# Output projection in plain 4608-byte runs with its input re-placed by small copies, and V units evacuated in pairs, in a gated attention + MLP decode kernel

## The chip, the cores and the metric

The kernel runs on one core of a Trainium2 chip. The metric is the device time of one execution in microseconds, as a median of runs of the same kernel. The profile shown is of one execution on the same kind of core; its times are counted from the first instruction of the span.

## What is computed

For eight batch rows with one token each (D = 576), the reference mixes an attention branch and an MLP branch by a gate:

```python
g = _sigmoid((x * gate_w).sum(-1, keepdims=True))
# attention: 32 query heads, 16 K/V heads, last W = 2048 of 8192 positions, Dh = 128
q = (x @ wq).reshape(B, 1, 32, 128)
p = softmax(q . k[:, :, -W:, :] * Dh ** -0.5)
a = (p . v[:, :, -W:, :]).reshape(B, 1, 4096) @ wo
b = _gelu(layernorm(x) @ w1 + b1) @ w2 + b2      # F = 4608
return g * a + (1 - g) * b
```

All tensors are bf16. The K and V windows are 67 MB each, wq, wo, w1 and w2 some 20 MB together.

## The kernel before

All data lives in one SBUF arena, addressed by hand. Operations aren't emitted where they are written: `add` and `dma` only record them, with an engine, dependencies (`deps`: wait until done; `after`: not started earlier), a cost in us and a priority. `_Plan.schedule` (L62) is a list scheduler: among all operations whose predecessors are planned it takes the one with the smallest planned start minus 0.2 us per unit of priority, then the higher priority, then the earlier recorded. So each engine's instruction order is fixed before the run, from these costs, and at run time every engine works through its own list in order and waits on semaphores.

All large loads go through SP's queue in one fixed order, each behind the one before (`after=last_dma`). First wq and w1. Then the order string (L553) interleaves 16 K units (4 MB), 32 V units (2 MB) and the four chunks of wo; b2 and four chunks of w2 follow. A load waits for its buffer: K units alternate between slots 0-1 and 2-3, V units and w2 chunks go round slots 4 to 8, and wo's four chunks take slots 0 to 3 when K is through (L735).

A K unit (L629) holds 512 positions of 32 (batch, K/V head) rows: two batch rows with all 16 heads, which make a G. Its two halves are transposed by VectorE in 32x32 blocks (L652) into two KT buffers, and TensorE multiplies them by the queries (L664) into 32 rows of PSUM. After four K units (one G complete), two softmaxes (`softmax`, L582) run, g = 2G and 2G+1: a row maximum (L586), its merging over the four partition quadrants by tiny copies (L589 to L595), the exponential on ScalarE with row sums (L597), four masked copies (L604), four block transposes into PT (L612), and then the row sums: a diagonal (L615), a matmul that adds over partitions (L616), the reciprocal (L618) and the product with the gate, rg (L623).

A V unit (L680, `v_compute` L687) holds all 2048 positions of four (batch, K/V head) rows: heads n and n + 8 of two batch rows. `pv` (L695) makes 16 matmuls of 512 columns, cycling over four column tiles of 32, into one of two PSUM banks. ScalarE copies the bank to SBUF (`uev`, L704). A selection (`us`, L710), four fp32 matmuls against a piece of an identity matrix (each shows as two instructions), adds the tiles' diagonal blocks and leaves the output with the head dimension on partitions. Two units make an item: ScalarE copies its result (L720), and GpSimd (for the last item VectorE) multiplies by rg and writes oT (L731), laid out by K/V head.

The output is accumulated in one PSUM bank by groups (`AccGroup`, L535) of matmul pairs of 288 columns in two column tiles (L544): `project` (L744) takes oT against wo, `m2_chunk` (L758) the MLP's hidden values against w2. When all groups are done, VectorE and ScalarE each take half out of PSUM (L790, L791) and two small DMAs write it (L793).

The lines that the change and the prediction touch are `softmax`, `k_unit`'s end, `v_compute`, `wo_chunk`, `project`, `m2_chunk` and the loop over the stream.

Of the kernel before, what the change touches and what calls it, by code (L numbers as in the profile page):

```python
# [181 lines left out]
def build_kernel(nc, A_x, A_k_cache, A_v_cache, A_wq, A_wo, B_x, B_w1, B_b1, B_w2, B_b2, gate_w, out):  # L182
# [13 lines left out]
    FC, FJ = 4, 9  # L196
# [10 lines left out]
    with ExitStack() as es:  # L207
# [22 lines left out]
        req("sel", 4 * 128, BF)  # L230
# [3 lines left out]
        req("qT", 256, BF)  # L234
# [14 lines left out]
        req("EV", 2 * 512, F32)  # L249
        req("oT", Hkv * 16, BF)  # L250
# [12 lines left out]
        over("xg", "P", 0, D, F32)  # L263
        over("xc", "KT", 0, D, F32)
# [25 lines left out]
        i32 = view("i32")  # L290
        idf8 = view("idf8", 8)
# [20 lines left out]
        oT = view("oT").rearrange("p (u h b) -> p u h b", u=Hkv, h=2)  # L312
# [139 lines left out]
        o_i32 = []  # L452
        for q in range(4):
            o_i32.append(add("dve", (lambda q=q: lambda e: e.tensor_copy(i32[32 * q:32 * q + 32, :], ident[32 * q:32 * q + 32, 32 * q:32 * q + 32]))(),
                             deps=[o_ident, o_obl], name="i32_%d" % q, cost=0.15, prio=-1))
# [79 lines left out]
        class AccGroup:  # L535
            def __init__(self, name, mms, deps, cost, after=(), prio=0):
# [3 lines left out]
                def fn(e):  # L540
# [13 lines left out]
                 "w w v v w w v v v v v v")  # L554
        count = {"K": 0, "V": 0, "W": 0}
        stream = []
        for word in order.split():
            kind = "V" if word == "v" else "W" if word == "w" else "K"
            stream.append((kind, count[kind]))
            count[kind] += 1  # L560
        assert (count["K"], count["V"], count["W"]) == (NKU, NUQ, Hq // WO_CH)
        stream += [("B", 0)] + [("M", i) for i in range(FC)]
# [19 lines left out]
        def softmax(g):  # L582
# [16 lines left out]
            exp_done[g] = [ex]  # L599
            pms = []  # L600
# [14 lines left out]
            ds = add("dve", lambda e: e.tensor_scalar(out=dsum, in0=i32, scalar1=k(S), scalar2=None, op0=ALU.mult), deps=[ex] + o_i32 + ([rg_done[g - 1]] if g else []), name="ds_%d" % g, cost=0.16, prio=5)  # L615
            sp_ = add("pe", lambda e: e.matmul(ps[:, BK_S, 0:32], ones_f, dsum, start=True, stop=True), deps=[ds] + b6_r[-2:], after=b6_w[-1:], name="sum_pe%d" % g, cost=0.5, prio=5)  # L616
            b6_w.append(sp_)
            rc = add("dve", lambda e: e.reciprocal(out=rr, in_=ps[:, BK_S, 0:32]), deps=[sp_], name="rc_%d" % g, cost=0.16, prio=5)  # L618
            b6_r.append(rc)

            def rg_fn(e):
                in1 = bass.AP(arena_f, offset=foffs("gb") + 2 * (g // 2), ap=[[AST // 2, 128], [0, 4], [1, 2], [0, 4]])
                return e.tensor_tensor(out=rg[:, g % 2, :].rearrange("p (v b m) -> p v b m", v=4, b=2), in0=rr.rearrange("p (v b m) -> p v b m", v=4, b=2), in1=in1, op=ALU.mult)  # L623
            deps = [rc, o_gb]
            if g >= 2:
                deps.append(oT_done[4 * (g - 2) + 3])
            rg_done[g] = add("dve", rg_fn, deps=deps, name="rg_%d" % g, cost=0.16, prio=5)

        def k_unit(i):  # L629
# [18 lines left out]
            for h in range(2):  # L648
# [5 lines left out]
                         deps=deps, name="tr%d_%d" % (i, h), cost=5.0, after=tr_hist[-1:])  # L654
# [21 lines left out]
            if c == 3:  # L676
                softmax(2 * G)
                softmax(2 * G + 1)
# [8 lines left out]
        def v_compute(i, s, d):  # L687
            g, q = divmod(i, 4)
            item = 2 * g + q // 2

            def pv_fn(e):
                mm = None
                for t in range(16):
                    c = 32 * (t % 4)
                    mm = e.matmul(ps[c:c + 32, BK_OS[i % 2], :], PT[:, g % 2, 512 * q + 32 * t:512 * q + 32 * t + 32], slot(s)[:, 512 * t:512 * t + 512],  # L695
                                  start=(t < 4), stop=(t >= 12), skip_group_check=True, tile_position=(0, c))
                return mm
            deps = [d] + pt_done[g] + ([u_ev[i - 2]] if i >= 2 else o_qT + [o_u])
            prev = add("pe", pv_fn, deps=deps, name="pv%d" % i, cost=1.5, after=pv_hist[-1:])
            pv_hist.append(prev)  # L700
            slot_free[s] = [prev]
            if q == 3:
                pv_last[g] = prev
            u_ev[i] = add("act", lambda e: e.activation(out=EV[:, i % 2, :], in_=ps[:, BK_OS[i % 2], :], func=ACTF.Copy),  # L704
                          deps=[prev] + ([u_sum[i - 2]] if i >= 2 else [o_hT]), name="uev%d" % i, cost=0.8, prio=3)

            def us_fn(e):
                mm = None
                for r in range(4):
                    mm = e.matmul(ps[:, BK_S, OC + 16 * (item % 2) + 8 * (q % 2):OC + 16 * (item % 2) + 8 * (q % 2) + 8], EV[:, i % 2, 128 * r:128 * r + 128], i32[:, 8 * r:8 * r + 8],  # L710
                                  start=(r == 0), stop=(r == 3), skip_group_check=True)
                return mm
            u_sum[i] = add("pe", us_fn, deps=[u_ev[i]] + o_i32 + b6_r[-2:], after=b6_w[-1:], name="us%d" % i, cost=1.0, prio=3)
            b6_w.append(u_sum[i])
            if q % 2 == 1:
                hl = q // 2
                prev = u_sum[i]
# [8 lines left out]
                for t in (i - 1, i):  # L726
                    G, n = divmod(t, 8)

                    def om_fn(e, t=t, G=G, n=n):
                        dst = bass.AP(arena, offset=aoffs("oT") + 16 * n + 2 * G, ap=[[AST, 128], [1, 2], [128, 2], [8, 2]])  # L730
                        return e.tensor_tensor(out=dst, in0=src_[:, 8 * (t % 2):8 * (t % 2) + 8].rearrange("p (b l h) -> p b l h", b=2, l=2),  # L731
                                               in1=rg[:, g % 2, 8 * (t % 4):8 * (t % 4) + 8].rearrange("p (b l h) -> p b l h", b=2, l=2), op=ALU.mult)
                    oT_done[t] = add(eng, om_fn, deps=deps, name="oT%d" % t, cost=0.25, prio=9)

        def wo_chunk(i):  # L735
            s = i
            h0 = WO_CH * i
            dst = slot(s)[:, 0:WO_CH * WOP].rearrange("p (t c) -> p t c", t=WO_CH)
            d = dma("sp", lambda e: e.dma_start(dst[:, :, 0:D], A_wo[128 * h0:128 * (h0 + WO_CH), :].rearrange("(t p) c -> p t c", p=128)),
                    "s%d" % s, WO_CH * 128 * D * 2, deps=slot_free[s], name="d_wo%d" % i, after=last_dma[-1:])  # L740
            last_dma.append(d)
            wo_here.append((dst, d))

        def project():  # L744
            for n in range(8):
                for hkv in (n, n + 8):
                    dst, d = wo_here[2 * hkv // WO_CH]
                    mms = [(oT[:, hkv, h, :], dst[:, 2 * hkv % WO_CH + h, 0:D]) for h in range(2)]
                    AccGroup("proj%d" % hkv, mms, [oT_done[n + 8 * m] for m in range(4)] + [d], cost=0.5)
# [8 lines left out]
        def m2_chunk(ci):  # L758
# [5 lines left out]
            for n, (j0, j1) in enumerate(zip(cuts, cuts[1:])):  # L764
# [6 lines left out]
                ops.append(AccGroup("m2_%d_%d" % (ci, n), mms, [o_hT, d], cost=0.25 * (j1 - j0), after=o_m2[-1:]).op)  # L771
# [4 lines left out]
        v_here, wo_here = [], []  # L776
        for kind, i in stream:
# [3 lines left out]
            while v_here and v_here[0][0] // 4 in pt_done:  # L781
                v_compute(*v_here.pop(0))
# [74 lines left out]
```

## Time and profile before

| What | us |
|---|---|
| Median of 5 runs | 367.7 |
| Lowest and highest | 366.93, 370.26 |
| The profiled execution | 367.76 |
| Its span, first to last instruction | 366.5 |
| PE busy (matmul) | 259.9 |
| VectorE busy | 210.9 |
| ScalarE busy | 31.0 |
| GpSimd busy | 17.4 |

In the rows by slice, each figure stands for a fortieth of the span (9.2 us); a digit is a busy share in tenths. A group line gives a source line, an engine, an operation, its destination and source with their shapes, the count, then the busy time in us and the mean of one in ns, then how long the engine was idle just before and what ended that. PE is the matmul stream, PEld the loading of weights, SPq and ACTq the queues from which DMAs are issued, POOL is GpSimd. Clock 1.0 is the full TensorE clock and 0.5 half of it.

### The profile page before, as it was taken

The numbers are of one execution on the slowest core, as the hardware profiler recorded it, in microseconds if no ns is written. First come the engines' busy times: TensorE is split into PE (matmuls) and PEld (weight loads), VectorE is DVE, ScalarE is ACT, GpSimd is POOL, SyncE is SP. The second block draws the span as 40 slices with busy tenths as digits, with TensorE's granted clock in tenths as the row PEclk, the third lists the DMA queues.
The fourth block names the chain that finished last, engine by engine and source line by source line (L and its number), as shares of the span: only waits on it lengthen the run. The fifth ranks groups of instructions, "written<-read, shape, count | busy, mean of one in ns | idle before, by whom it ended". The sixth has DMA issues, their size and how long they took to land.

```text
span 366.5 us, 4165 instructions
## 1 busy us (share of the span) xinstructions
PE 259.9 (71%) x1805; PEld 133.9 (37%) x1805; DVE 210.9 (58%) x255; ACT 31.0 (8%) x69; POOL 17.4 (5%) x80
## 2 busy tenths in 40 slices
PE   0179684847589959466899293748999497368997
PEld 0169331312255424222544141213744233126555
DVE  0610986575997490869954442779854836960000
ACT  1010000000210000002100000002100100021110
POOL 4012000001000000010000000000000000000000
PEclk9999999669698967696969768586769788755579
DMA  9999999999999999999999999999999999999994
GB/s 403 429 425 410 426 431 449 415 446 415 445 424 434 426 431 440 424 445 413 451 420 436 426 433 424 443 418 442 420 452 422 442 379 436 401 432 433 426 427 181
DMA packets 12618, 154.58 MB, mean 422 GB/s; under 512 B 1036, under 2 KB 5300, under 8 KB 5816
## 3 DMA queue, kind: packets, MB, share of 16 engines
q1 hardware_dynamic: 12544, 154.29, 98.9%
q8 instruction: 14, 0.23, 0.2%
q10 hardware_dynamic: 56, 0.03, 0.0%
q14 instruction: 4, 0.03, 0.0%
HBM read 154.31 MB, written 0.01 MB: 421 GB/s over the span
## 4 chain that ended last, share of the span: by engine, by line
DMA 40%; PE 29%; DVE 28%; issue 1%; SPq 1%; ACT 1%; DVEq 0%
DMA arena<-in_A_k_cache_dram 35%; DVE arena L652 16%; PE ps L664 14%; PE ps L710 8%; DVE arena L612 6%; DMA arena<-in_A_v_cache_dram 4%; PE ps L695 4%; PE ps L544 2%; DVE arena L604 2%; DVE arena L586 1%; DVE arena L595 1%; DVE arena L589 1%; SPq L683 1%; ACT arena L704 1%; DVE arena L618 0%
## 5 line engine op out<-in xcount | busy, mean ns | idle before, releaser
L652 DVE STREAM_TRANSPOSE arena<-arena 128x4096 f32<-128x4096 f32 x32 | 141.1, 4431 | 84.7 <-DMA arena<-in_A_k_cache_dram 75.8
L664 PE MATMUL ps<-arena 128*32 128x512 bf16 x512 | 141.4, 441 | 37.0 <-DVE arena L652 36.9
L664 PEld LDWEIGHTS ps<-arena 128*32 128x32 bf16 x512 | 51.2, 105 | 118.8 <-DVE arena L652 43.0
L695 PE MATMUL ps<-arena 128*32 128x512 bf16 x512 | 57.0, 542 | 28.7 <-DMA arena<-in_A_v_cache_dram 15.7
L710 PE MATMUL ps<-arena 128*128 128x8 f32 x256 | 41.3, 293 | 6.8 <-ACT arena L704 3.3
L710 PEld LDWEIGHTS ps<-arena 128*128 128x128 f32 x256 | 39.1, 238 | 19.0 <-issue 6.8
L695 PEld LDWEIGHTS ps<-arena 128*32 128x32 bf16 x512 | 19.5, 123 | 50.5 <-issue 28.7
L612 DVE STREAM_TRANSPOSE arena<-arena 128x512 bf16<-128x512 bf16 x32 | 30.6, 1015 | 0.0
L704 ACT ACTIVATE arena<-ps 128x512 f32<-128x512 f32 x32 | 19.1, 596 | 124.8 <-PE ps L695 90.7
L731 DVE TENSOR_TENSOR arena<-ps,arena 128x8 bf16<-128x8 f32 x2 | 0.3, 188 | 30.4 <-PE ps L710 30.4
L731 POOL TENSOR_TENSOR arena<-arena 128x8 bf16<-128x8 f32 x30 | 5.8, 231 | 239.9 <-ACT arena L720 239.9
L597 ACT ACTIVATE arena<-ps,arena 128x512 bf16<-128x512 f32 x8 | 5.5, 688 | 115.2 <-DVE arena L595 115.2
L616 PE MATMUL ps<-arena 128*128 128x32 f32 x16 | 3.9, 334 | 12.8 <-DVE arena L615 12.8
L586 DVE TENSOR_REDUCE arena<-ps 128x1 f32<-128x512 f32 x8 | 5.5, 692 | 13.0 <-PE ps L664 12.9
L501 PE MATMUL ps<-arena 128*128 128x8 bf16 x144 | 10.9, 201 | 1.7 <-DMA arena<-in_B_w_dram 1.7
L544 PE MATMUL ps<-arena 128*8 128x288 bf16 (+1 forms) x140 | 12.0, 316 | 0.0
L501 PEld LDWEIGHTS ps<-arena 128*128 128x128 bf16 x144 | 10.8, 157 | 2.1 <-DMA arena<-in_B_w_dram 2.1
L645 POOL TENSOR_TENSOR arena<-arena 128x32 bf16<-128x32 bf16 x32 | 6.4, 239 | 81.0 <-PE ps L664 72.0
L604 DVE TENSOR_SCALAR arena<-arena 128x512 bf16<-128x512 bf16 x32 | 9.0, 345 | 1.0 <-ACT arena L597 0.8
L616 PEld LDWEIGHTS ps<-arena 128*128 128x128 f32 x16 | 3.0, 234 | 17.1 <-DVE arena L615 15.7
L419 PE MATMUL ps<-arena 8*128 8x8 bf16 x8 | 0.6, 171 | 11.9 <-DVE arena L392 7.9
L544 PEld LDWEIGHTS ps<-arena 128*8 128x8 bf16 (+1 forms) x140 | 6.1, 92 | 4.6 <-issue 2.2
(81 smaller groups left out, 78.0 us busy)
## 6 DMA issues: line engine op xcount, KB each, us to landing
arena<-in_A_k_cache_dram SPq DMA_DIRECT2D x16, 4096.0 KB, 23.9
arena<-in_A_v_cache_dram SPq DMA_DIRECT2D x32, 2048.0 KB, 23.8
arena<-in_B_w_dram SPq DMA_DIRECT2D x1, 4608.0 KB, 23.8
arena<-in_A_wo_dram SPq DMA_DIRECT2D x4, 1152.0 KB, 10.6
arena<-in_A_wq_dram SPq DMA_DIRECT2D x1, 4096.0 KB, 13.2
arena<-in_B_w_dram SPq DMA_DIRECT2D x3, 1296.0 KB, 14.5
arena<-in_B_w_dram SPq DMA_DIRECT2D x3, 576.0 KB, 9.3
arena<-in_A_wq_dram SPq DMA_DIRECT2D x1, 512.0 KB, 3.3
```

What stands on the lines that cost most here:

```text
L501: ins = e.matmul(out_, lhsT, yT[:, kt, :], start=(kt == 0), stop=False)
L544: ins = e.matmul(ps[32 * j:32 * j + 8, BK_ACC, 0:JN], lhsT, rhs[:, JN * j:JN * j + JN], start=False, stop=True, skip_group_check=True, til ...
L586: mx = add("dve", lambda e: e.tensor_reduce(out=k(MX), in_=ps[:, bank, :], axis=AXL.X, op=ALU.max), deps=[qk_done[g]], name="mx%d" % g, co ...
L604: return e.tensor_scalar(out=dst, in0=view("Pd").rearrange("p (s n) -> p s n", s=2), scalar1=amask[:, a:a + 1], scalar2=None, op0=ALU.mult)
L612: return e.transpose(dst, src)
L616: sp_ = add("pe", lambda e: e.matmul(ps[:, BK_S, 0:32], ones_f, dsum, start=True, stop=True), deps=[ds] + b6_r[-2:], after=b6_w[-1:], name ...
L645: return e.tensor_tensor(out=dst, in0=src, in1=own, op=ALU.mult)
L652: tr = add("dve", (lambda h=h, kb=kb: lambda e: e.transpose(bass.AP(arena_f, offset=foffs("KT") + kb * SE // 2, ap=[[AST // 2, 128], [4, 1 ...
L664: mm = e.matmul(ps[32 * c:32 * c + 32, 2 * (G % 2) + nb, :], qb[:, G % 2, n, 2 * h + ee, :], rhs, start=(h == 0 and t == 0), stop=(h == 1 ...
L695: mm = e.matmul(ps[c:c + 32, BK_OS[i % 2], :], PT[:, g % 2, 512 * q + 32 * t:512 * q + 32 * t + 32], slot(s)[:, 512 * t:512 * t + 512], st ...
L704: u_ev[i] = add("act", lambda e: e.activation(out=EV[:, i % 2, :], in_=ps[:, BK_OS[i % 2], :], func=ACTF.Copy), deps=[prev] + ([u_sum[i - ...
L710: mm = e.matmul(ps[:, BK_S, OC + 16 * (item % 2) + 8 * (q % 2):OC + 16 * (item % 2) + 8 * (q % 2) + 8], EV[:, i % 2, 128 * r:128 * r + 128 ...
```

## The change

Wo. A chunk's 1024 rows were read as 1152-byte rows, each partition taking one row from each of eight blocks of 128. Now partition p takes four consecutive rows (4608 bytes) from each of two blocks of 512, so that partition p's row j of block c is row 512 c + 4 p + j. The contraction over a head's 128 dimensions thus no longer lies with dimension on partitions, and the attention output has to be re-placed: the products are first written to oN, and 16 copies per step, one for each pair of partition quadrants, move pieces of 32 partitions into the new oT. One such step handles all that is there after unit 23, and one each follows units 25, 27, 29 and 31 (80 copies in all, on VectorE). The projection becomes 8 groups of four matmul pairs instead of 16 groups of two.

V. The two units of an item share a PSUM bank: the first takes column tiles 0 and 1, the second 2 and 3, so that each unit cycles over two tiles. One ScalarE copy, now reading PSUM with a stride, and one selection with 16 columns (against a new constant, i2) serve both.

Softmax. The row-sum operations are recorded ahead of the masked copies and transposes (now `spread`). Softmaxes go through a list, `waiting`. Some planned costs change, and qT and sel move into another buffer's space. The order of the stream stays the same.

```diff
-        req("sel", 4 * 128, BF)
+        req("i2", 64, F32)
...
+        req("oN", Hkv * 16, BF)
...
+        o_i20 = add("dve", lambda e: e.memset(view("i2"), 0.0), name="i2z", cost=0.1, prio=-1)
+        o_i2 = [add("dve", (lambda q=q: lambda e: e.tensor_copy(i2[32 * q:32 * q + 32, :, q // 2, :], ident[32 * q:32 * q + 32, 32 * q:32 * q + 32].rearrange("p (r m) -> p r m", r=4)))(),
+                    deps=[o_i20, o_ident], name="i2_%d" % q, cost=0.15, prio=-1) for q in range(4)]
...
             exp_done[g] = [ex]
+            ds = add("dve", lambda e: e.tensor_scalar(out=dsum, in0=i32, scalar1=k(S), scalar2=None, op0=ALU.mult), deps=[ex] + o_i32 + ([rg_done[g - 1]] if g else []), name="ds_%d" % g, cost=0.16, prio=5)
+            sp_ = add("pe", lambda e: e.matmul(ps[:, BK_S, 0:32], ones_f, dsum, start=True, stop=True), deps=[ds] + b6_r[-2:], after=b6_w[-1:], name="sum_pe%d" % g, cost=0.5, prio=5)
+            b6_w.append(sp_)
+            rc = add("dve", lambda e: e.reciprocal(out=rr, in_=ps[:, BK_S, 0:32]), deps=[sp_], name="rc_%d" % g, cost=0.16, prio=5)
+            b6_r.append(rc)
...
+        def spread(g):
+            ex = exp_done[g][0]
             pms = []
...
-                         deps=deps, name="tr%d_%d" % (i, h), cost=5.0, after=tr_hist[-1:])
+                         deps=deps, name="tr%d_%d" % (i, h), cost=4.5, after=tr_hist[-1:])
...
                 for t in range(16):
-                    c = 32 * (t % 4)
-                    mm = e.matmul(ps[c:c + 32, BK_OS[i % 2], :], PT[:, g % 2, 512 * q + 32 * t:512 * q + 32 * t + 32], slot(s)[:, 512 * t:512 * t + 512],
-                                  start=(t < 4), stop=(t >= 12), skip_group_check=True, tile_position=(0, c))
+                    c = 64 * (i % 2) + 32 * (t % 2)
+                    mm = e.matmul(ps[c:c + 32, bk, :], PT[:, g % 2, 512 * q + 32 * t:512 * q + 32 * t + 32], slot(s)[:, 512 * t:512 * t + 512],
+                                  start=(t < 2), stop=(t >= 14), skip_group_check=True, tile_position=(0, c))
                 return mm
-            deps = [d] + pt_done[g] + ([u_ev[i - 2]] if i >= 2 else o_qT + [o_u])
-            prev = add("pe", pv_fn, deps=deps, name="pv%d" % i, cost=1.5, after=pv_hist[-1:])
+            deps = [d] + pt_done[g] + ([u_ev[item - 2]] if item >= 2 else o_qT + [o_u])
+            prev = add("pe", pv_fn, deps=deps, name="pv%d" % i, cost=1.9, after=pv_hist[-1:])
...
+            if i % 2 == 0:
+                return
+            u_ev[item] = add("act", lambda e: e.activation(out=EV[:, item % 2, :], in_=ps[:, bk, :].rearrange("p (r d j) -> p r j d", r=4, j=4), func=ACTF.Copy),
+                             deps=pv_hist[-2:] + ([u_sum[item - 2]] if item >= 2 else [o_hT]), name="uev%d" % item, cost=1.2, prio=3)
...
-            u_sum[i] = add("pe", us_fn, deps=[u_ev[i]] + o_i32 + b6_r[-2:], after=b6_w[-1:], name="us%d" % i, cost=1.0, prio=3)
+            u_sum[item] = add("pe", us_fn, deps=[u_ev[item]] + o_i2 + b6_r[-2:], after=b6_w[-1:], name="us%d" % item, cost=1.9, prio=3)
...
+                if i == NUQ - 9:
+                    place(slice(0, 8), slice(0, 6), list(oT_done.values()))
+                elif i >= NUQ - 8:
+                    c = (i % 8) // 2
+                    place_done[c] = place(slice(c, 8, 4), slice(6, 8), [oT_done[i - 1], oT_done[i]])
+
+        place_done = {}
+
+        def place(ch, bs, deps):
+            return [add("dve", (lambda j=j, q=q: lambda e: e.tensor_copy(oT[32 * q:32 * q + 32, ch, j, bs], oN[32 * j:32 * j + 32, q, ch, bs]))(), deps=deps, name="pl%d%d" % (j, q), cost=0.1, prio=2)
+                    for j in range(4) for q in range(4)]
...
-            dst = slot(s)[:, 0:WO_CH * WOP].rearrange("p (t c) -> p t c", t=WO_CH)
-            d = dma("sp", lambda e: e.dma_start(dst[:, :, 0:D], A_wo[128 * h0:128 * (h0 + WO_CH), :].rearrange("(t p) c -> p t c", p=128)),
+            dst = slot(s)[:, 0:WO_CH * D].rearrange("p (c n) -> p c n", c=2)
+            src = A_wo[128 * WO_CH * i:128 * WO_CH * (i + 1), :].rearrange("(c p j) n -> p c (j n)", c=2, j=4)
+            d = dma("sp", lambda e: e.dma_start(dst, src),
...
-            for n in range(8):
-                for hkv in (n, n + 8):
-                    dst, d = wo_here[2 * hkv // WO_CH]
-                    mms = [(oT[:, hkv, h, :], dst[:, 2 * hkv % WO_CH + h, 0:D]) for h in range(2)]
-                    AccGroup("proj%d" % hkv, mms, [oT_done[n + 8 * m] for m in range(4)] + [d], cost=0.5)
+            for c in range(4):
+                for ch in (c, c + 4):
+                    dst, d = wo_here[ch // 2]
+                    mms = [(oT[:, ch, j, :], dst[:, ch % 2, D * j:D * j + D]) for j in range(4)]
+                    AccGroup("proj%d" % ch, mms, place_done[c] + [d], cost=1.0)
...
-                ops.append(AccGroup("m2_%d_%d" % (ci, n), mms, [o_hT, d], cost=0.25 * (j1 - j0), after=o_m2[-1:]).op)
+                ops.append(AccGroup("m2_%d_%d" % (ci, n), mms, [o_hT, d], cost=0.16 * (j1 - j0), after=o_m2[-1:]).op)
...
-            while v_here and v_here[0][0] // 4 in pt_done:
-                v_compute(*v_here.pop(0))
+            while True:
+                if waiting and (waiting[0] < 2 or waiting[0] - 2 in pv_last):
+                    softmax(waiting[0])
+                    spread(waiting.pop(0))
+                elif v_here and v_here[0][0] // 4 in pt_done:
+                    v_compute(*v_here.pop(0))
+                else:
+                    break
```

## The prediction

> **What bounds the kernel now.** I read the page first: span, the rows by slice, the queues.
>
> ```profile
> span 366.5 us, 4165 instructions
> ...
> DMA  9999999999999999999999999999999999999994
> GB/s 403 429 425 410 426 431 449 415 446 415 445 424 434 426 431 440 424 445 413 451 420 436 426 433 424 443 418 442 420 452 422 442 379 436 401 432 433 426 427 181
> ...
> q1 hardware_dynamic: 12544, 154.29, 98.9%
> ```
>
> The 16 DMA engines are busy 98.9% of the span with one queue, SP's, and the bytes (154 MB) don't change. Only three things can move the end: the rate at which bytes flow, a hole in the stream, and what follows the last byte. The GB/s row has two dips late, 379 and 401: there Wo is read. Busy time by stretch (columns: PE, PEld, DVE, ACT, POOL busy, PE clock, DMA share, GB/s) with Wo's second half in the first row and V loads in the second:
>
> ```profile
> 312.60:318.60 6.00, 1.31 (x5) 0.60 (x3) 5.65 (x20) 0.78 (x2) 0.00 (x0) 0.77 1.03 381
> 318.60:328.60 10.00, 6.07 (x50) 2.20 (x50) 8.21 (x22) 1.86 (x4) 0.00 (x0) 0.50 1.03 433
> ```
>
> The engines are equally busy and move 12% less. Then the end, in the chain of waits (start us, us, what):
>
> ```profile
> 353.11 0.61 ACT arena L704
> 353.71 0.04 issue
> 353.76 1.06 PE ps L710 x8
> ...
> 356.57 0.61 ACT arena L704
> 357.18 0.04 issue
> 357.22 1.06 PE ps L710 x8
> 358.28 6.29 PE ps L544 x96
> ...
> 364.59 0.45 DVE arena L790
> ```
>
> PE is the last link: 96 accumulation matmuls (L544) run without a gap from 358.28 to 364.57. The trace's landing times say that the last piece of w2 is there at 363.15. So PE ends 1.42 us behind the data, working off a backlog left by the last V units. Last, the prices:
>
> ```profile
> L664 PE MATMUL ps<-arena 128*32 128x512 bf16 x512 | 141.4, 441 | 37.0 <-DVE arena L652 36.9
> L695 PE MATMUL ps<-arena 128*32 128x512 bf16 x512 | 57.0, 542 | 28.7 <-DMA arena<-in_A_v_cache_dram 15.7
> L710 PE MATMUL ps<-arena 128*128 128x8 f32 x256 | 41.3, 293 | 6.8 <-ACT arena L704 3.3
> ```
> ```profile
> 312.23 0.49 DVE L589 COPY arena<-arena 32x1 f32<-32x1 f32 x3
> 320.27 3.60 PE L695 MATMUL ps<-arena 128*32 128x512 bf16 x32 [3.15 <-DVE arena L612]
> ```
>
> 57.0/32 = 1.8 us per V unit for L695, 41.3/32 = 1.3 us for L710. Three tiny DVE copies take 0.49, starts 0.175 apart.
>
> [...] a 1152-byte packet takes 51 ns, a 4608-byte one (in w2's last chunk) 178, not 204. [...] at full clock, sixteen 512-column matmuls over four column tiles (L695) take 1.04 us at 100.9, while eight in one tile (L664) take 1.98. [...] The clock records have just 0.5 and 1.0, in steps of 3.4 us; it rose at 309.0 in an unbroken run of L664, but stayed half from 315.8 to 353.4 although PE looked busy from 331 on, mixing L695 and L710. [...]
>
> **The change, part by part.** The sum is made against the profiled execution, 367.76 us (span 366.48 and 1.28 around it), 0.06 above the median of 367.7.
>
> *Wo in 4608-byte runs.* Packets 4096 -> 1024. By landing times, the four chunks add 12.1 us to the stream (K15 299.76, Wo 302.76 and 305.78; V25 315.47, Wo 318.48 and 321.55). A 589,824-byte piece of w2 in 4608-byte packets adds 1.38 us (360.03 to 361.41, again to 362.79); Wo holds eight such: 11.04. **Gain 1.04 us.** Packet durations give more, (4096 x 51 - 1024 x 178)/16 = 1.66 us, but packets overlap a little on an engine; landings decide, 1.66 stays as the other end. The stream is one fixed SP order, so all later landings move up by 1.04: V31 350.87 -> 349.8, last w2 piece 363.15 -> 362.1. Shorter descriptor lists also free SP's issue (V24's took 4.75 us, V26's 3.17, after Wo): worth nothing, 10.7 and 8.9 us were queued ahead.
>
> *PV in two column tiles per unit instead of four.* Eight rounds replace four: the eight-in-one-tile row L664 is the price, 1.98 us full clock, 3.62 half (1.04 and 1.90 before). 32 units: +30 us at full clock, +55 at half. *One evacuation and selection per pair*: 16 selections of 8 matmuls go, 16 x 1.06 = -17 us at full clock, -30 at half; 16 columns instead of 8 cost nothing, weights being loaded for 128 (PEld 238 ns of the 293). 16 evacuations of 0.60 us go. Net on PE +13 to +25 us in 366, where it is 71% busy; hidden in the body by DMA, and worth anything only where a slot is freed late. Smallest covers: K6 issued at 111.49 with 7.3 us still to land ahead, w2's last chunk at 353.10 with 6.9. Without cover each us late costs a us. The strided evacuation isn't in this trace: between 0.60 (same elements) and 1.20 (twice), below 0.60 excluded since as many elements are read; I take 0.60.
>
> *Row sums ahead of the masking.* The reciprocal now stands before the transposes on DVE and waits for a PE matmul that queues behind PV; behind it wait the mask products, transposes and K's next transpose, hence K's next load. Bound 0 to one or two PV units (3.6 us half clock each) per softmax, no gain on the path; covers above: zero. It also lets selection 12 go before the last transposes; in the profile it waited for the reciprocal at 327.66 and then behind V27's landing. New i2 operations run in DVE's empty first 30 us.
>
> *Placing.* 80 copies on DVE. The first 16, behind pair 11, fall near 299, where K15's transpose starts: 16 x 0.175 = 2.8 us late at most. That pushes Wo's third load (issued 308.58, 6.9 us of cover): zero. The last 16 stand in the tail: 2.8 us.
>
> *Tail.* V24 can start at about 321.0 (320.3, plus reciprocal and product ahead of the transposes). [...] PE then waits for V landings. After V31 (349.8): PV 2.8 (mean of both clocks), evacuation 0.7, selection 1.47 (mean of 1.06 and 1.88): 354.8. Then 0.14 to DVE, two products 0.27, copies 2.8, last projection 8 pairs x 0.12 = 1.0 and 0.1 of waits: 359.1. w2's third chunk lands at 359.0 and takes 1.1, the fourth's pieces land at 360.4, 361.75, 362.1: the second takes 0.5, the last pair 0.12 and 0.3 to end: **362.7**. Before 364.57: gain 1.87, of which 1.04 is DMA and 0.83 the backlog. What is late next is the data itself.
>
> 367.76 - 1.87 = **365.9 us**.
>
> **Rivals.** *Transfer only*: copies and PV keep PE as far behind as now; 367.76 - 1.04 = 366.7. For: 2.8 us of new copies in the tail. Against: 16 selection matmuls fewer there. *More*: packet times are right and the backlog goes with a full clock, 1.66 + 0.9: 365.2. *PE ends it* (slower): the clock stays half, as it did from 315.8 to 353.4. From 321.0, 8 PV x 3.62, 4 selections x 1.88, two evacuations x 0.7, and 22 accumulation pairs x 0.24 make 43.2 us; 32.4 are done by 353.4, the rest at full clock takes 5.4: selection 15 ends at 358.8. With 0.4 of products, 2.9 of copies and wait, 1.0 of projection and 2.5 for the two chunks: 365.6, +1.0, 368.8; the clock a window later adds 1.7: 370.5. Point 369.7. It decides from a selection that ends after 357.7. For: the clock row[...].
>
> **Numbers.** Forecast 0.48, its own range 365.2 to 366.6; transfer only 0.15; more 0.20; PE ends it 0.17. 0.5% of 367.7 is 1.84 us, about what a measurement of this kernel can tell from no change; the forecast lies on that line, so it splits: faster 0.25, same 0.23. With "more" faster, "transfer only" same, and "PE ends it" slower 0.15, same 0.02: 0.45, 0.40, 0.15. Range 364.8 (1.66, and the lag down from 1.42 to the 0.4 that the last two matmuls need, 365.1, less 0.3 for scatter between runs) to 368.9 (PE with the clock as before).
>
> **What would show it.** Four Wo loads of 4608-byte packets at about 427 GB/s; last landing about 362; PE's last run of L544 with gaps waiting for DMA; L695's busy time near 100 us, L710's near 21; sixteen DVE copies taking about 2.8 us before the last projection. Wrong if landings move by less than 0.7 or more than 1.7 us, if the DMA row shows a hole near Wo or w2, or if PE still runs its last matmuls without a gap.

## The result, and the profile after

| | before | changed |
|---|---|---|
| Median of runs | 367.8 (76 runs) | 366.7 (39 runs) |
| Lowest, highest | 366.9, 370.5 | 366.0, 368.6 |
| Profiled execution, span | 367.76, 366.5 | 366.08, 364.8 |
| Last landing of w2, PE's end (from the span's start) | 363.15, 364.55 | 362.46, 362.87 |

The ratio of the times is 0.9972 (95% interval 0.9961 to 0.9983): 1.1 us less, inside the range on record, 0.8 above the forecast. The profiled execution gained 1.68 us, nearly the 1.87 forecast. The gap between these two gains is one of the things that the experiments are about.

The page of the changed kernel, the same rows as before:

```profile
span 364.8 us, 3973 instructions
...
DMA  9999999999999999999999999999999999999995
GB/s 398 434 398 444 410 451 428 435 439 411 453 411 450 411 444 426 424 438 426 438 424 438 422 438 426 434 429 431 433 437 438 422 414 439 426 431 428 429 424 217
...
q1 hardware_dynamic: 9472, 154.29, 98.9%
```

The stream is as full as before, with 3072 packets fewer, and the dip to 379 is gone. By stretch (columns as in the prediction), Wo's second half, then V loads:

```profile
315.00:320.70 5.70, 0.64 (x4) 0.53 (x6) 5.61 (x15) 0.00 (x0) 0.00 (x0) 0.55 1.06 443
320.70:330.60 9.90, 8.34 (x58) 3.88 (x58) 6.86 (x21) 1.56 (x4) 0.39 (x2) 0.74 1.00 427
```

Wo now moves no slower than V. Packets are cut off at the edges of such a short stretch, so the landings give the amount: Wo's loads added 5.53 us (299.83 to 305.36) and 5.63 us (315.03 to 320.66), 11.16 together instead of 12.1. The costliest groups that changed:

```profile
L707 PE MATMUL ps<-arena 128*32 128x512 bf16 x512 | 60.6, 450 | 22.9 <-DVE arena L598 18.8
L724 PE MATMUL ps<-arena 128*128 128x16 f32 x128 | 16.9, 264 | 5.2 <-ACT arena L718 3.5
L757 DVE COPY arena<-arena 32x4 bf16<-32x4 bf16 (+1 forms) x80 | 12.9, 161 | 11.5 <-POOL arena L745 9.4
```

PV (L695 before) has 60.6 us instead of 57.0, the selection 16.9 instead of 41.3. The end, in the timeline (start us, us, engine, line, what, in brackets the idle time before it and what ended that):

```profile
350.03 1.90 PE L707 MATMUL ps<-arena 128*32 128x512 bf16 x16 [0.15 <-DMA arena<-in_A_v_cache_dram]
...
351.97 0.60 ACT L718 ACTIVATE arena<-ps 128x512 f32<-128x512 f32 x1 [7.74 <-PE ps L707]
...
353.12 1.27 PE L551 MATMUL ps<-arena 128*8 128x288 bf16 x18 [0.85 <-DMA arena<-in_B_w_dram]
...
354.32 1.06 PE L724 MATMUL ps<-arena 128*128 128x16 f32 x8
...
355.72 3.03 DVE L757 COPY arena<-arena 32x4 bf16<-32x4 bf16 x16
...
358.80 2.74 PE L551 MATMUL ps<-arena 128*8 128x288 bf16 x42 [1.30 <-DVE arena L757]
...
362.09 0.78 PE L551 MATMUL ps<-arena 128*8 128x288 bf16 x10 [0.55 <-DMA arena<-in_B_w_dram]
```

Before, PE ran 96 accumulation matmuls without a gap. Now each block waits for something: w2's chunks, then the copies, and the last ten matmuls for w2's last pieces. PE ends 0.41 us behind the data instead of 1.40 (1.42 in the prediction, where PE's end is that of the chain of waits, 364.57), and the chain's last DMA link is now the load of w2:

```profile
348.13 13.92 DMA arena<-in_B_w_dram
...
362.09 0.80 PE ps L551 x10
```

Look at the order too: the evacuation of the last pair is done at 352.57, yet its selection starts at 354.32. It stands behind w2's first chunk, which waits for its landing.

A load lands in sixteen pieces, and "last landing" means the last piece. Of w2's last load the first piece is there 2.95 us ahead of the last in the kernel before, and 3.10 us in the changed one: the end hangs on the latest of sixteen.

### The profile page after: what moved, and what is told of

Its sections match the earlier page's. It is cut to its first block, busy times and chain, and to the rows that moved or that the text cites. A ratio compares the mean times of both kernels' runs of the same rounds, so it can differ in the third digit from the quotient of the medians.

```text
span 364.8 us, 3973 instructions
## 1 busy us (share of the span) xinstructions
PE 241.9 (66%) x1677; PEld 116.5 (32%) x1677; DVE 226.2 (62%) x340; ACT 22.4 (6%) x53; POOL 17.4 (5%) x80
## 4 chain that ended last, share of the span: by engine, by line
DMA 63%; DVE 26%; PE 8%; issue 1%; SPq 0%; DVEq 0%
DMA arena<-in_A_k_cache_dram 54%; DVE arena L662 20%; PE ps L674 6%; DMA arena<-in_A_v_cache_dram 5%; DMA arena<-in_B_w_dram 4%; DVE arena L635 3%; PE ps L707 2%; DVE arena L627 1%; DVE arena L593 1%; DVE arena L596 0%; DVE arena L602 0%; DVE arena L610 0%; PE ps L551 0%; DVE arena L607 0%; PE ps L608 0%
## 5 line engine op out<-in xcount | busy, mean ns | idle before, releaser
L674 PE MATMUL ps<-arena 128*32 128x512 bf16 x512 | 142.1, 441 | 61.4 <-DVE arena L662 61.4
L674 PEld LDWEIGHTS ps<-arena 128*32 128x32 bf16 x512 | 52.4, 106 | 143.8 <-DVE arena L662 66.5
L707 PE MATMUL ps<-arena 128*32 128x512 bf16 x512 | 60.6, 450 | 22.9 <-DVE arena L598 18.8
L707 PEld LDWEIGHTS ps<-arena 128*32 128x32 bf16 x512 | 24.7, 109 | 48.9 <-issue 31.0
L724 PE MATMUL ps<-arena 128*128 128x16 f32 x128 | 16.9, 264 | 5.2 <-ACT arena L718 3.5
L757 DVE COPY arena<-arena 32x4 bf16<-32x4 bf16 (+1 forms) x80 | 12.9, 161 | 11.5 <-POOL arena L745 9.4
L724 PEld LDWEIGHTS ps<-arena 128*128 128x128 f32 x128 | 15.5, 191 | 11.1 <-ACT arena L718 8.9
L718 ACT ACTIVATE arena<-ps 128x512 f32<-128x512 f32 x16 | 9.6, 598 | 153.2 <-PE ps L707 153.2
L508 PE MATMUL ps<-arena 128*128 128x8 bf16 x144 | 10.9, 201 | 1.8 <-DMA arena<-in_B_w_dram 1.8
L510 PE MATMUL ps<-arena 128*128 128x8 bf16 x36 | 7.2, 201 | 0.0
```

Source lines behind the costliest of these rows:

```text
L508: ins = e.matmul(out_, lhsT, yT[:, kt, :], start=(kt == 0), stop=False)
L510: ins = e.matmul(out_, lhsT, yT[:, 4 + c // 2, :], start=False, stop=True)
L674: mm = e.matmul(ps[32 * c:32 * c + 32, 2 * (G % 2) + nb, :], qb[:, G % 2, n, 2 * h + ee, :], rhs, start=(h == 0 and t == 0), stop=(h == 1 ...
L707: mm = e.matmul(ps[c:c + 32, bk, :], PT[:, g % 2, 512 * q + 32 * t:512 * q + 32 * t + 32], slot(s)[:, 512 * t:512 * t + 512], start=(t < 2 ...
L718: u_ev[item] = add("act", lambda e: e.activation(out=EV[:, item % 2, :], in_=ps[:, bk, :].rearrange("p (r d j) -> p r j d", r=4, j=4), fun ...
L724: mm = e.matmul(ps[:, BK_S, OC + 16 * (item % 2):OC + 16 * (item % 2) + 16], EV[:, item % 2, 128 * r:128 * r + 128], i2[:, r, :, :].rearra ...
```

## The experiments

Two theories were put against each other. *Data and lag*: the end is the last landing plus PE's lag behind it; Wo moves the landing, the rest of the change the lag. *Transfer*: Wo is all that counts. The first results raised a further question: why do the runs of one kernel fall into groups of times, and is it the stream of loads or an *exposed tail*, a chain of steps behind the last V unit that nothing covers any more? The table has the profiled execution of each kernel (a single run: last landing, lag and time) and the median of all its runs. The kernel before was run beside the experiments in three sets, with medians of 367.93, 367.94 and 367.95; each ratio is to the runs beside it.

| kernel | last landing | lag | its time | median (runs) | ratio to before |
|---|---|---|---|---|---|
| before | 363.15 | 1.40 | 367.76 | 367.8 (76) | |
| e13 before again | 363.36 | 1.44 | 368.10 | 368.1 (1) | |
| e1 Wo's runs only | 362.57 | 1.25 | 367.03 | 366.84 (20) | 0.997 (0.9955 to 0.9985) |
| e8 pairs only | 363.36 | 0.46 | 367.04 | 367.07 (10) | 0.9969 (0.9947 to 0.9992) |
| e2 changed, rows back | 363.28 | 0.47 | 366.96 | 367.32 (22) | 0.9984 (0.9968 to 0.9999) |
| changed | 362.46 | 0.41 | 366.08 | 366.70 (39) | 0.9972 (0.9961 to 0.9983) |
| e7 changed, again | 362.38 | 1.35 | 366.93 | 366.61 (20) | 0.997 (0.9958 to 0.9983) |
| e3 changed, units apart | 364.64 | 3.37 | 371.20 | 369.80 (22) | 1.0043 (1.0025 to 1.006) |
| e11 e3, no tail copies | 362.70 | 0.95 | 366.85 | 366.82 (20) | 0.9974 (0.9962 to 0.9986) |
| e4 changed, sums late | 362.47 | 0.47 | 366.15 | 366.15 (12) | 0.9947 (0.993 to 0.9964) |
| e5 changed, no tail copies | 362.55 | 1.24 | 367.01 | 366.26 (4) | 0.9958 (0.9943 to 0.9974) |
| e6 selection first | 362.49 | 0.46 | 366.16 | 366.26 (4) | 0.9955 (0.994 to 0.997) |
| e12 selection first, again | 362.28 | 0.46 | 365.93 | 366.22 (22) | 0.996 (0.9949 to 0.9972) |
| e9 selection first and fill | 363.44 | 3.35 | 370.03 | 366.78 (12) | 0.9984 (0.9963 to 1.0005) |

The four profiles with the old rows have their last landing at 363.15 to 363.36. Of the ten with Wo in long runs, eight have it at 362.28 to 362.70, on average 0.80 us earlier. The other two, e3 and e9, have one late piece each: in e3 fifteen of the sixteen pieces of w2's last load are there by 362.43 and one comes at 364.64, in e9 by 362.60 and at 363.44.

**e1, Wo's runs only.**

```diff
-            dst = slot(s)[:, 0:WO_CH * WOP].rearrange("p (t c) -> p t c", t=WO_CH)
-            d = dma("sp", lambda e: e.dma_start(dst[:, :, 0:D], A_wo[128 * h0:128 * (h0 + WO_CH), :].rearrange("(t p) c -> p t c", p=128)),
+            dst = slot(s)[:, 0:WO_CH * D].rearrange("p (t c) -> p t c", t=WO_CH)
+            src = A_wo[128 * h0:128 * (h0 + WO_CH), :].rearrange("(c p j) n -> p c (j n)", c=2, j=4)
+            d = dma("sp", lambda e: e.dma_start(slot(s)[:, 0:WO_CH * D].rearrange("p (c n) -> p c n", c=2), src),
```

> The kernel before with one edit: Wo's four loads read 4608-byte runs. The projection's input is not re-placed, so the output projection multiplies heads by the wrong rows of Wo (same amount of work). Data theory (the end follows the stream of bytes plus a lag of PE behind the last landing; Wo's runs shorten the stream by about 0.95 us, and the rest of the change takes the lag from 1.4 to 0.4): Wo's two pairs of loads take 11.1 us of the stream instead of 12.1, the last landing comes 0.9 to 1.0 earlier than before, PE still ends 1.2 to 1.5 behind it; median 366.8, 0.95 under before. Transfer theory (Wo is all that counts, the lag costs nothing): median as the changed kernel's, 366.7, 1.1 under before, and no difference between the two in any part of their distributions.

Measured 366.84. Wo's loads take 11.05 us of the stream, the landing is 0.58 earlier in the profile, and PE's last stretch is the old one, only sooner, in the chain of waits:

```profile
357.55 6.29 PE ps L544 x96
```

So the transfer gain comes alone, and most of the lag stays (1.25). By medians, e1 and the changed kernel are hardly apart, which the transfer theory would have.

**e2, the changed kernel with Wo's old rows.**

```diff
-            src = A_wo[128 * WO_CH * i:128 * WO_CH * (i + 1), :].rearrange("(c p j) n -> p c (j n)", c=2, j=4)
-            d = dma("sp", lambda e: e.dma_start(dst, src),
+            src = A_wo[128 * WO_CH * i:128 * WO_CH * (i + 1), :].rearrange("(t p) n -> p t n", p=128)
+            d = dma("sp", lambda e: e.dma_start(slot(s)[:, 0:WO_CH * D].rearrange("p (t n) -> p t n", t=WO_CH), src),
```

> The changed kernel with Wo read in 1152-byte rows again (everything else, copies included, stays; rows of Wo then meet the wrong dimensions in the output projection). Data theory: the stream is 0.95 us longer again, PE still ends 0.4 behind the last landing, so the median is 367.6 or so: 0.9 over the changed kernel and 0.1 to 1.0 under before. Transfer theory: nothing is left of the gain, 367.8 like before. A third view, that the pairing frees PE and so speeds up the stream itself: the last landing would come earlier than in the kernel before.

Measured 367.32; the landing is back at 363.28 and the lag stays at 0.47. The profiled executions of e2 and the changed kernel differ by 0.88 us, 0.82 of it in the landing. That speaks for data and lag and against transfer alone: without it 0.0016 of the time is still gained, though only just clear of zero (interval 0.0001 to 0.0032). e8 below is the stronger case.

**e3, V units apart**, with the pv, uev and us code of the kernel before inside the changed one:

```diff
-                    c = 64 * (i % 2) + 32 * (t % 2)
+                    c = 32 * (t % 4)
...
-            if i % 2 == 0:
-                return
```

> The changed kernel with V units one by one as before: four column tiles, one evacuation and one selection of 8 columns each (same result as the reference's). Data theory: PE has 16 selections more in the tail region only in part, the lag behind the last landing comes back to between 0.6 and 1.4 us, median 366.9 to 367.5; the clock falls to half for longer than in the changed kernel and L695-like matmuls cost 1.5 us and more a unit. Transfer theory: 366.7, like the changed kernel. If the lag stays at 0.4 here, it was the order of row sums or the planned costs that took the backlog away, not the pairing.

A miss of both: 369.8, slower than the kernel before. Its chain of waits:

```profile
350.42 1.13 PE ps L551 x8
...
356.73 1.07 PE ps L720 x8
357.83 0.28 DVE arena L741 x2
...
360.99 0.17 DVE arena L753
361.21 6.82 PE ps L551 x70
```

The last selection ends at 357.8 instead of 355.4; then products, copies until 361.2, and 70 matmuls that all stand behind them. This is the slower rival of the prediction ("from a selection that ends after 357.7"), in another kernel. The late piece of its last load is not what makes it late: PE works without a gap from 361.21 to 368.0, 5.6 us past the other fifteen.

**e11, e3 without its last 64 copies.**

```diff
-                    place_done[c] = place(slice(c, 8, 4), slice(6, 8), [oT_done[i - 1], oT_done[i]])
+                    place_done[c] = list(oT_done.values())
...
-                    mms = [(oT[:, ch, j, :], dst[:, ch % 2, D * j:D * j + D]) for j in range(4)]
+                    mms = [(oN[:, j, ch, :], dst[:, ch % 2, D * j:D * j + D]) for j in range(4)]
```

> The kernel with V units apart (e3, 369.8) without its last 64 placing copies (projection on the old layout, wrong rows of Wo). If the copies, which there have no cover, are what made it slower than the kernel before, it falls by about their 3 us: 366.5 to 367.2, the time of the kernel before with Wo's runs alone. If the selections themselves are what is too much for PE, it stays above 368.5.

Measured 366.82: three microseconds less. The copies, where nothing covers them, cost what they take. And it is as fast as e1 (366.84), which also has the units apart and Wo in long runs: the early row sums and the new planned costs, which e11 has and e1 hasn't, together bring nothing without the pairing.

**e4, row sums late**: the block from `ds` to `rg_done` moved to the end of `spread`.

> The changed kernel with the row sums recorded after the transposes again. Data theory: selection 12 waits for the reciprocal after softmax 7's transposes again (near 328 instead of 325) and PE starts its last stretch 2 to 4 us later, but with V landings still to wait for the lag at the end grows by 0 to 0.6 us: 366.7 to 367.3. Transfer theory: 366.7. DVE no longer waits for the row-sum matmul between the mask products.

Measured 366.15, better than the changed kernel, where 0 to 0.6 us worse was expected. Moving the sums also changed the planned order at the far end: here the last selection stands ahead of w2's first chunk and starts at 352.68. That gave the idea of e6, which moves the selection alone.

**e7, the changed kernel again.**

> The changed kernel itself once more on the chip of the others of this call. Both theories: median 366.1 to 366.9, and the profile, if it falls on a run over 367.2, shows where the time goes: exposed tail, a late last selection or half clock after 353 and PE ending over 2 us behind the last landing; stream, a last landing 1 us or more later with PE 0.4 behind it.

Median 366.61 (20 runs, 366.03 to 368.44). Its profile is of a run of 366.93; a run over 367.2 wasn't profiled. The last landing is at 362.38, as early as in the first profile, and the lag is 1.35. Busy time from 355.3 to 362.1, first in this run, then in the first profile:

```profile
355.30:362.10 6.80, 5.70 (x49) 2.83 (x50) 2.82 (x18) 0.00 (x0) 0.00 (x0) 0.50 0.76 307
```
```profile
355.30:362.10 6.80, 4.10 (x63) 2.55 (x64) 2.82 (x18) 0.00 (x0) 0.00 (x0) 1.00 0.77 312
```

At half clock, PE gets 14 matmuls fewer done in the same time. From this run's timeline:

```profile
354.26 1.07 PE L724 MATMUL ps<-arena 128*128 128x16 f32 x8
356.16 2.32 PE L551 MATMUL ps<-arena 128*8 128x288 bf16 x18 [0.83 <-DMA arena<-in_B_w_dram]
358.75 4.99 PE L551 MATMUL ps<-arena 128*8 128x288 bf16 x52 [0.27 <-DVE arena L757]
```

18 matmuls take 2.32 instead of 1.27, and everything behind the copies (52 matmuls) runs without a gap to the end, as before the change. The stream is not what makes this run later; the tail is. The mean clocks of the twenty runs fit: 0.841 to 0.860 in the ten up to 366.43, 0.827 to 0.837 in the eight from 366.79 to 367.28. But the two slowest, 368.04 and 368.44, have 0.842, and of the eleven over 367.5 among the changed kernel's 39 runs eight have 0.842 to 0.851. A lower clock is not what sets these apart, and neither theory is shown for them.

**e5, the changed kernel without its last 64 copies** (the edit of e11, in the changed kernel).

> The changed kernel without the last 64 placing copies; the projection reads the products where they lie, in the old layout, so it multiplies by the wrong rows of Wo (the first 16 copies stay, unread). Exposed-tail theory (the changed kernel's runs at 367.2 to 368.6, a third of them, come from the chain last selection, products, 3 us of copies, projection, two w2 chunks, which ends late when the clock falls to half[...]): without the copies the chain ends 3 us sooner and these runs go; all runs at 366.0 to 366.9, median 366.1 to 366.3. Stream theory (they come from the DMA engines, some runs ending their last bytes later): a third of the runs stays above 367.2 and the median is 366.6 or so.

Median 366.26 (four runs, 366.07 to 367.01): none over 367.2, but one at 367.01, and the profile is that one. Without any copy in the tail its lag is 1.24; the clock was at half from 350.7 to 361.0. So a late tail doesn't need the copies, it came with the half clock alone. Four runs are few to say how often. e5 differs from e11 in the pairing only, and is 0.56 us faster by medians. That is what the pairing brings by itself, with Wo in long runs, as far as four runs and intervals that overlap can say.

**e6 and e12, the last selection first.**

```diff
-            u_sum[item] = add("pe", us_fn, deps=[u_ev[item]] + o_i2 + b6_r[-2:], after=b6_w[-1:], name="us%d" % item, cost=1.9, prio=3)
+            u_sum[item] = add("pe", us_fn, deps=[u_ev[item]] + o_i2 + b6_r[-2:], after=b6_w[-1:], name="us%d" % item, cost=1.9, prio=15 if item == Hkv - 1 else 3)
```

> The changed kernel with one priority raised, so that the last selection stands before w2's first chunk and the bias on PE instead of behind them (nothing else in any engine's order differs). Exposed-tail theory: in the changed kernel that selection waits for the landing of w2's first chunk and its 18 matmuls (it starts at 354.3 though its evacuation ends at 352.6); going first, the chain is 1.6 us earlier and most of the runs over 367.2 go: median 366.1 to 366.4. Stream theory: no change, 366.6 with a third of the runs above 367.2.

> The kernel with the last selection first once more, for its time: 366.1 to 366.4 with no run above 367, 0.3 to 0.5 us under the changed kernel's median and 1.5 to 1.8 under the kernel before. Stream theory: 366.6, a third of the runs above 367.2.

The order of every engine but PE is unchanged, and on PE only this selection moved. e6 gave 366.26 (4 runs), e12 366.22 (22 runs, three of them over 366.6, against 22 of 39 for the changed kernel). One run, at 367.04, is over the 367 that was expected not to be passed. e6's timeline:

```profile
352.64 1.06 PE L724 MATMUL ps<-arena 128*128 128x16 f32 x8 [0.69 <-ACT arena L718]
353.64 1.61 PE L551 MATMUL ps<-arena 8*8 8x288 bf16 x22
356.30 5.49 PE L551 MATMUL ps<-arena 128*8 128x288 bf16 x60 [1.05 <-DMA arena<-in_B_w_dram]
362.17 0.78 PE L551 MATMUL ps<-arena 128*8 128x288 bf16 x10 [0.38 <-DMA arena<-in_B_w_dram]
```

The selection starts as its evacuation ends. The clock was at half from 356.3 to 359.7 here too, but with the chain 1.7 us earlier the last ten matmuls still wait for data: lag 0.46. In e7 the half clock lasted from 355.3 to 362.1, twice as long, so these two profiles alone don't separate the earlier chain from the shorter half clock. The times do show what the order is worth: the 26 runs of e6 and e12 have a median of 366.23, the 59 of the changed kernel (with e7) 366.70, 0.47 us apart (0.1 to 0.7 in 95% of resamplings of the runs). Of the 59, 13 lie over 367.5, of the 26 none. This version beats both kernels.

**e8, pairs only**: the kernel before with the pairing, the early row sums and the new planned costs; Wo's rows, oT and the projection as before.

> The kernel before with the pairing, the order of row sums and the planned costs of the change, but Wo in 1152-byte rows, the old layout of the projection's input and no placing. Additive view (Wo 0.95, lag 1.0, both in the profile): last landing as before, about 363.2, PE 0.4 to 0.5 behind it, profile span 365.5, median 366.9 and hardly a run above 367.3, since there is no chain of copies to be exposed. Transfer theory: 367.8, as before.

367.07, nine of ten runs within 366.90 to 367.15, one at 367.77. Landing 363.36, lag 0.46, as the additive view had it; PE's last ten matmuls wait for w2:

```profile
349.08 13.92 DMA arena<-in_B_w_dram
...
363.05 0.80 PE ps L552 x10
```

**e9, selection first and fill**: 4, 8 and 4 matmuls into a free PSUM bank behind w2's first three chunks.

```diff
...
+                        mm = e.matmul(ps[0:32, 0, 0:288], view("hT")[:, 0:32], view("hT")[:, 0:288], start=True, stop=True, skip_group_check=True, tile_position=(0, 0))
...
```

> The kernel with the last selection first (e6) plus 16 idle matmuls of 288 columns into a free PSUM bank, 4, 8 and 4 of them behind w2's first three chunks, so that PE has less idle time while it waits for landings. Exposed-tail theory, in its form that a half clock in the last 10 us is what a late tail needs: if the fill keeps the clock at 1.0, the lag stays at 0.4 to 0.5 and all runs lie at 366.0 to 366.4. If PE's idle time isn't what halves the clock, it still falls in some runs and the fill then costs up to 2 us at half clock: some runs at 367 and above. Stream theory: as e6.

366.78 (12 runs, nine at 366.6 to 366.85, one at 370.03, ratio 0.9984, 0.9963 to 1.0005). The fill costs half a microsecond by medians. In the profiled run, that of 370.03, the clock was at half from 356.2 to 363.1, although PE had worked 3.8 of the 4.5 us before that. But the first fill matmul starts at 356.27, just after the clock had fallen (356.23). So this run does not tell whether filling the pauses holds the clock, and what drops it stays open.

**e13, the kernel before again.**

> The kernel before once more, one look. Its times lie in two groups, 366.9 to 367.5 and 367.6 to 368.4 (and a few at 370). Exposed-tail theory: the last landing is at 363.1 to 363.4 in either group; if this run falls in the lower one, the clock is at 1.0 for more of the stretch from 316 to 353 and PE ends about 0.5 behind the last landing; in the upper one, 1.2 or more behind. Stream theory: the groups differ in the last landing, by 0.8.

One run, 368.1, of the upper of the two groups: landing 363.36, lag 1.44, clock at half from 315.9 to 353.4, as in the first profile. The lower group was not profiled, so the question that this run was for stays open.

## Why the prediction came out as it did

**Wo in 4608-byte runs: right, slightly over.** 1.04 was forecast from landings (its own figures, 12.10 - 11.04, give 1.06), 0.94 measured on Wo's loads (1.05 in e1). The forecast passed it on whole to the last landing, which moved by 0.69 in the two first profiles, 0.58 in e1 and 0.80 on average over the profiles above. The other end, 1.66 from packet times, was wrong. The floors agree: the lowest time is 366.9 for the three kernels with old rows (before, e2, e8) and 365.9 to 366.1 for e1, the changed kernel, e4 and e12, which have new ones.

**PV in two tiles: the term was wrong in sign.** Forecast +13 to +25 us on PE; PE's busy time fell by 18 us (259.9 to 241.9). The selections fell by 24.4, within the forecast of 17 to 30, but PV rose by 3.6 where 30 to 55 were forecast (L695 "near 100"). The price of a unit that runs alone was right, 1.90 us at full clock (1.98 forecast) and 3.60 at half. Two things failed. The forecast charged each unit at one clock on both sides: before, 10 of 32 units ran wholly at full clock and 19 at half, now 20 and 5, and the mean clock rose from 0.804 to 0.846. For the tail the prediction took the mean of both clocks (PV 2.8, selection 1.47); that the clock would rise there was its author's estimate, and the sum left a rise out. What makes the clock rise is not shown by these runs. And the forecast counted each unit alone, though two units that follow each other have different column tiles (0 and 1, then 2 and 3) and overlap, as here the fourth and the fifth:

```profile
107.39 1.93 PE L707 MATMUL ps<-arena 128*32 128x512 bf16 x24
```

That is 24 matmuls of the two in 1.93 us, where the sixteen of the last unit, alone, take 1.90 (at 350.03). The wrong sign had no visible consequence for the time: as the prediction said, the body is covered by the DMA stream. The strided evacuation took 0.60 us, as assumed.

**Copies: right size, half of the place wrong.** 3.03 us for the last 16 (2.8 forecast). The first 16 did not fall near 299 but at 308.55, behind K15's transposes, where they end at 311.41 and the next row maximum waits for PE until 311.58: zero, as forecast.

**Row sums: zero.** The cover held. Moving them back (e4) changed the last selection's place too, so e4 is to be set against e12, in which that selection also stands ahead of w2's first chunk: 366.15 and 366.22.

**The tail: the sum was right for one run, partly by luck, and a step of it failed.** Forecast 354.8 for the end of the last selection and 362.7 for PE's end; profiled 355.4 and 362.9. The gain is split otherwise than forecast, 0.69 from the landing and 0.99 from the lag instead of 1.04 and 0.83, and the two errors partly cancel. And the prediction put the selection straight behind its evacuation ("PV 2.8, evacuation 0.7, selection 1.47"). In the plan it stands behind w2's first chunk, and waits 1.7 us; that PV and selection ran at full clock (1.9 and 1.06) made up for most of it. What the step lost is the margin: in a run in which the clock drops near 355, the chain selection, copies, projection, two chunks ends about 1 us late (e7). The backlog's 0.83 was the right size for what the pairing brings by itself: e8 is 0.86 under the runs of the kernel before beside it (367.93). Of this gain and Wo's 0.94, the changed kernel keeps 1.1 to 1.3 by medians; with the selection first it keeps 1.7 (e12 366.22, the kernel before beside it 367.95), close to the 1.87 forecast. So the missing half microsecond is lost through the place of the last selection: e6 and e12 edit only that. That it is lost through a half clock in the tail is seen in one profile (e7) and in the mean clocks of the runs up to 367.3, not in the slower ones.

**Its signs of being right or wrong.** Wo's loads moved at 423 GB/s by landings (427 said), and the last landing, the gaps before PE's last matmuls and the copies came as said. L695 near 100 us and L710 near 21 did not (60.6 and 16.9). Two signs of being wrong were touched: the last landing moved by 0.69 in the first pair of profiles, just under the 0.7 that was named, and in e7 PE runs its last matmuls without a gap.

**The rivals.** *Transfer only* came nearest in time (366.7) and is not the mechanism: e2 and e8 gain without it. *More* didn't happen. *PE ends it* didn't happen in the changed kernel, where it would have needed a selection after 357.7; e3 shows it at 357.8 and pays 1.9 us over the kernel before.

**Left open**: what halves the clock in the last 10 us, and why; what makes the changed kernel's runs over 367.5 (11 of 39) late, and those of the kernel before at 370 (10 of 76), none of which was profiled. That the kernel before's lower group (366.9 to 367.5, 18 of the 63 runs beside e1) has no lag is argued from its floor and its higher clock (mean 0.825 against 0.814 in the group above), and was not seen in a profile.

## What to carry to other kernels

When a stream of loads sets the end, the time is its last landing plus the lag of what consumes it: read both from the profile, and price a transfer by the distance of landings, not by packet times (1.06 and 1.66 us here, 0.94 measured). A change that adds steps behind the last data needs cover for them that holds at half clock too (lag 0.41 in the first profile, 1.35 in e7 at half clock); here the pairing pays for the copies, and the copies without the pairing (e3) lose 1.9 us against the kernel before. In a planned instruction order, look up what the last step of the chain stands behind: one selection queued behind a wait for data cost some half a microsecond of the median.

## What the runs showed of the hardware

Packets of 1152 bytes took 51 ns, but landings put them only 47 ns apart on an engine ((305.78 - 299.76)/128); those of 4608 bytes took 178 and came 173 apart (1.38/8): durations overlap by 4 to 5 ns, a tenth of a small packet.

The page of the kernel before has 14 packets in q8 and 4 in q14, two queues of kind instruction, taken here for program fetches. Data packets of 16,384 bytes took 0.61 us; in the kernel before, nine of 4096 took 0.83 to 1.16, and each of the nine starts within 1 us after a fetch of 16 or 8 KB. There are 14 fetches of 16 KB in its span and 13 in the changed kernel's.

The sixteen pieces of one load don't land together: the first and last are 1.4 us apart at 25 us and 3.0 us apart at the end of the kernel before.

SP's next issue behind a pair of Wo's loads took 4.7 to 4.8 us and 3.2 us in the kernels with 1152-byte rows (before, e2, e8), and in e1, the changed kernel and e12, which have 4608-byte runs, no issue of a load after 290 us took over 1 us. The stream had no hole there in either case: the DMA share is 0.99 to 1.06 in the stretches from 297 to 320 us, before and after. That the issue is worth nothing was right.

A busy PE did not bring the full clock in one stretch of the kernel before: it stayed at half from 315.8 to 353.4, with PE busy for 96% of the time from 335.0 on.

At full clock, sixteen matmuls of 512 columns took 1.04 us over four column tiles (before) and 1.90 over two (changed), and units over different pairs of tiles overlapped: 24 matmuls in 1.93.

A copy of 32 partitions by four bf16 values took 0.16 us, with starts 0.19 apart, a little more than L589's one-element copies in the kernel before (0.14 and 0.175), whose distance had priced it. ScalarE's copy of 128x512 fp32 values out of PSUM took 0.60 us both contiguous (before) and with a stride of four elements (changed).
